# One transformer layer on one core: dense sums read out by two engines, reciprocals over 128 rows

## The chip, the core and the metric

The kernel runs on one core of a Trainium2 chip. A core has a matrix engine (TensorE, PE in the profile; its weight loads are PEld), a vector engine (VectorE, DVE), a scalar engine (ScalarE, ACT), GpSimd (POOL) and SyncE (SP), which issues the transfers here. Matrix products land in PSUM, eight banks of 128 x 512 numbers of four bytes. The metric is the device time of one execution in microseconds (us). Before the change the median of three runs was 1553.09 us (1552.69 to 1554.96).

## The reference: what is computed

A layer with attention and a feed-forward part side by side, for 2048 tokens of width 512:

```python
def _A_ref(x, wqkv, wo):
    qkv = (x @ wqkv).reshape(B, S, 3, H, Dh)...      # 32 heads of 16
    scores = einsum("bhqd,bhkd->bhqk", q, k) * (Dh ** -0.5)
    o = einsum("bhqk,bhkd->bhqd", softmax(scores), v)
    return o... @ wo

def _B_ref(x, w1, b1, w2, b2):                       # 512 -> 1792 -> 512
    h = gelu(einsum("bsd,df->bsf", x, w1) + b1)      # tanh form
    return einsum("bsf,fd->bsd", h, w2) + b2

xn = layernorm(x)
return x + _A_ref(xn, wqkv, wo) + _B_ref(xn, w1, b1, w2, b2)
```

## The kernel before, in words

**Attention.** Work is cut into *units* (`unit`). A tile t is one group of 4 heads and one block of 512 queries, 32 tiles in all; it has 16 units, 512 in all. A unit makes, for four heads, one 128 x 512 block of scores twice. `s_half` computes scores with queries on rows, and VectorE takes their row maximum (`mt`, L250). `e_half`, 20 units later, computes them with keys on rows and the maximum folded in, and ScalarE takes the exponential (`pe`, L295). `v_half` multiplies the exponentials with the values (`pV`). So a unit costs VectorE four maxima and ScalarE four exponentials. At the end of a tile `s_end` turns the maxima into two rows for the next step (L261, L271, L272), and `v_end` copies the sums out (`osb`, L321, ScalarE); their denominators go to memory and come back spread over rows (`dn`), VectorE takes reciprocals (L339), and they return, spread over the rows of `rb`, for GpSimd to multiply.

**Banks.** The scores for the maxima go round through three PSUM banks (tag S), those for the exponentials through three (T). One bank holds the running sums of a dense product (D) and one those of the values (V). At the end of a dense product its bank joins the T banks, and the next product takes one of theirs. TensorE can write a bank only after its reader is through.

**The feed-forward part** is fitted into the units as *groups* of dense products (`Group`, `dense`), each ending in one 128 x 512 block of sums in one bank. There are four blocks of 512 tokens. Each has 14 groups of the first layer (12 products each; by turns 4 units and 3 units long), whose sums VectorE reads out, scaled and with the bias, as `hh` (L992); GpSimd and ScalarE make the gelu of it (`gelu`; the tanh is L961, ScalarE). Then come 4 groups of the second layer (42 products each, 14 units long; 12 in the last block), whose sums ScalarE reads out, scaled, as `yt` (L1008); GpSimd adds them up. In all there are 56 readouts `hh` and 16 `yt`. In the trace the first layer of block 0 runs from 316 to 441 us and its second layer up to 587 us.

**Order.** Each engine works through its list in the order in which the program writes it (`manual_schedule` over all five engines). `later(n, ...)` puts a piece of work n units further on; `pooled` feeds GpSimd's list at a fixed pace per unit. A group's end (`ended`) is written right after the half unit that brought its last product. Waits between engines are put in by the layer below the kernel, from which tiles an instruction reads and writes. `given` only keeps a count which nothing reads.

Of the kernel before, what the change touches and what calls it, by code (L numbers as in the profile page):

```python
# [8 lines left out]
F32 = mybir.dt.float32  # L9
F16 = mybir.dt.float16  # L10
I32 = mybir.dt.int32
AF = mybir.ActivationFunctionType
ALU = mybir.AluOpType
# [4 lines left out]
P = 128  # L18
# [25 lines left out]
W = 2 * P  # L44
# [3 lines left out]
def layer_kernel(ctx: ExitStack, tc: tile.TileContext, x, wqkv, wo, w1, b1, w2, b2, out):  # L48
    nc = tc.nc
# [3 lines left out]
    def pool(stack, name, bufs=1, space=None, side=None):  # L53
        kw = {k: v for k, v in (("space", space), ("side", side)) if v is not None}
        return stack.enter_context(tc.tile_pool(name=name, bufs=bufs, **kw))

    const = pool(ctx, "const")
    work = pool(ctx, "work")
# [11 lines left out]
    den_d = dram.tile([NG * NQB, 2, 4, QB], F32, name="den_d")  # L70
# [88 lines left out]
    def given(engine, ns):  # L159
        backlog[engine] += ns  # L160
# [43 lines left out]
    def later(n, fn, local=False):  # L204
        queue.append((slot[0] + n, fn, local))
# [10 lines left out]
    def pooled(*todo):  # L216
        steps.extend(todo)
# [93 lines left out]
    def v_end(u):  # L311

        t, kt = divmod(u, 16)
        g, qb = divmod(t, NQB)
        for h in range(4):
            del ptiles[u, h]
        if kt < 15:
            return
        pv, k = pv_of.pop(t)
        osb = work.tile([P, QB], F32, name="osb", bufs=2)  # L320
        nc.scalar.activation(osb, pv, AF.Copy)  # L321
        given("act", 600)
        free_banks["S"].append(k)
        if t == NG * NQB - 1:
            later(1, lambda: last_one(osb))
            return

        dn = work.tile([64, 32], F32, name="dn", bufs=1)
        rb = work.tile([P, QB], F32, name="rb", bufs=1)

        def sums():
            for h in range(4):
                nc.sync.dma_start(den_d[t, 0, h:h + 1, :], osb[32 * h + DH:32 * h + DH + 1, :])

        def turned():
            nc.sync.dma_start(dn, den_d[t, 0].rearrange("h (c q) -> (h c) q", q=32))

        def inverse():
            nc.vector.reciprocal(dn, dn)  # L339
            given("dve", 330)  # L340

        def keep():
            nc.sync.dma_start(den_d[t, 1].rearrange("h (c q) -> (h c) q", q=32), dn)

        def spread():
            for h in range(4):
                nc.sync.dma_start(rb[32 * h:32 * h + 32, :], den_d[t, 1, h:h + 1, :].to_broadcast([32, QB]))

        def store():
            ot = work.tile([P, 2, QB], F16, name="ot", bufs=2)  # L350
            pooled((1280, lambda: nc.gpsimd.tensor_tensor(osb, osb, rb, op=ALU.mult)),  # L351
                   (620, lambda: nc.gpsimd.tensor_scalar(ot[:, 0], osb, 1.0, 0.0, op0=ALU.mult, op1=ALU.add)),
                   (1160, lambda: nc.gpsimd.tensor_tensor(ot[:, 1], osb, ot[:, 0], op=ALU.subtract)),
                   (0, lambda: later(6 if t < (NG - 1) * NQB else 1, put)))

            def put():
                for h in range(4):
                    nc.sync.dma_start(ot_d[64 * g + DH * h:64 * g + DH * h + DH, :, qb * QB:(qb + 1) * QB],
                                      ot[32 * h:32 * h + DH])
                ready.add(t)  # L360


        at = (1, 3, 6, 7, 9, 12) if t < (NG - 1) * NQB else (1, 2, 5, 6, 7, 8)
        for k, fn in zip(at, (sums, turned, inverse, keep, spread, store)):
            later(k, fn)
# [168 lines left out]
    def fetch_x(b):  # L534
        if b < NQB:
            xbs[b] = feed[0].tile([P, 2, NC, QB], F16, name="xb", bufs=1)
            for c in range(NC):
                later(1 + c, lambda c=c: nc.sync.dma_start(xbs[b][:, :, c], xn_d[:, :, c, b * QB:(b + 1) * QB]))

    def fetch_w1(n):  # L540
        if n < NQB * NF:
            wcs[n] = feed[0].tile([P, 2, NC, P], F16, name="wc", bufs=3)
            nc.sync.dma_start(wcs[n], w1_d[n % NF // 2, :, n % 2])
# [91 lines left out]
    with ExitStack() as st1:  # L635
# [245 lines left out]
        gs = const.tile([P, 4], F32, name="gs")  # L881
# [69 lines left out]
    def mlp():  # L951
        m2 = st2p
        w2_s = m2.tile([P, 2, NF, D], F16, name="w2_s")
        b2_b = m2.tile([P, D], F32, name="b2_b")
        done = set()

        def gelu(hh, g, b, f):
            t1 = m2.tile([P, QB], F32, name="t1", bufs=2)

            def tanh():  # L960
                nc.scalar.activation(t1, t1, AF.Tanh, scale=GELU_C * GELU_A)  # L961
                given("act", 600)
                later(1, rest, True)

            def rest():
                pooled((690, lambda: nc.gpsimd.tensor_scalar(t1, t1, 1.0, gs[:, 1:2], op0=ALU.add, op1=ALU.mult)),
                       (1280, lambda: nc.gpsimd.tensor_tensor(t1, t1, hh, op=ALU.mult)),  # L967
                       (620, lambda: nc.gpsimd.tensor_scalar(g[:, 0, f, :], t1, 1.0, 0.0, op0=ALU.mult, op1=ALU.add)),
                       (1160, lambda: nc.gpsimd.tensor_tensor(g[:, 1, f, :], t1, g[:, 0, f, :], op=ALU.subtract)),  # L969
                       (0, lambda: done.add((b, f))))  # L970

            pooled((1040, lambda: nc.gpsimd.tensor_tensor(t1, hh, hh, op=ALU.mult)),  # L972
                   (620, lambda: nc.gpsimd.tensor_scalar(t1, t1, 1.0, 1.0 / GELU_A, op0=ALU.mult, op1=ALU.add)),
                   (1280, lambda: nc.gpsimd.tensor_tensor(t1, t1, hh, op=ALU.mult)),  # L974
                   (0, lambda: later(2, tanh, True)))

        for b in range(NQB):
            xb = xbs[b]
            g = m2.tile([P, 2, NF, QB], F16, name="g", bufs=1)
            for f in range(NF):  # L980
                later(1, lambda n=b * NF + f + 2: fetch_w1(n))
                wc = wcs[b * NF + f]
                if b == 0 and f >= 3:
                    for k in range(f - 3, NF if f == NF - 1 else f - 2):
                        later(2 * (k - f + 3), lambda k=k: nc.sync.dma_start(w2_s[:, :, k], w2_d[:, :, k]))
                if b == 0 and f == 3:
                    nc.sync.dma_start(b2_b, b2[None, :].to_broadcast([P, D]))

                def hidden(hp, g=g, b=b, f=f):
                    hh = m2.tile([P, QB], F32, name="hh", bufs=3)  # L990
                    scale, bias = fac1[0][:, f // 2:f // 2 + 1], b1_s[:, f:f + 1]
                    nc.vector.tensor_scalar(hh, hp, scale, bias, op0=ALU.mult, op1=ALU.add)  # L992
                    given("dve", 700)
                    later(1, lambda: gelu(hh, g, b, f), True)

                yield Group([lambda c=c, i=i, j=j, wc=wc, xb=xb: (wc[:, i, c, :], xb[:, j, c, :])
                             for c in range(NC) for i, j in PAIRS], dbank, hidden, pace=FAST if f % 2 else SLOW)
            for q in range(4):
                t = b * 4 + q
                xa = m2.tile([P, D], F32, name="xa", bufs=2)  # L1000
                if q == 1:
                    fetch_x(b + 1)
                nc.sync.dma_start(xa, x[t * P:(t + 1) * P, :])
                later(3, lambda xa=xa: pooled((1280, lambda: nc.gpsimd.tensor_tensor(xa, xa, b2_b, op=ALU.add))), True)

                def store(yp, xa=xa, t=t):
                    yt = m2.tile([P, D], F32, name="yt", bufs=2)
                    nc.scalar.activation(yt, yp, AF.Copy, scale=gs[:, 2:3])  # L1008
                    given("act", 600)
                    add = lambda: nc.gpsimd.tensor_tensor(xa, xa, yt, op=ALU.add)  # L1010
                    put = lambda: nc.sync.dma_start(acc_d[t * P:(t + 1) * P, :], xa)
                    later(1, lambda: pooled((1280, add), (0, lambda: later(4, put, True))), True)

                yield Group([lambda f=f, i=i, j=j, q=q, g=g: (g[:, i, f, q * P:(q + 1) * P], w2_s[:, j, f, :])
                             for f in range(NF) for i, j in PAIRS], dbank, store,
                            lambda n, b=b: (b, n // 3) in done, pace=SLOW if b < 3 else MEAN)
# [126 lines left out]
```

## Time and profile before

| | us |
|---|---|
| median of 3 runs | 1553.09 |
| profiled execution | 1552.32 |
| its span | 1550.5 |
| TensorE busy | 1509.9 (97%) |
| VectorE busy | 1423.0 (92%) |
| ScalarE busy | 1368.6 (88%) |
| GpSimd busy | 652.7 (42%) |

The granted TensorE clock was 0.998 over the span. A row of a timeline gives the start of the first instruction and the length of the whole row, in us from the span's start; then engine, line, operation, what it writes and reads, and how many instructions of one kind the row holds; in brackets, idle time of the engine before it and what ended that. Instructions of one engine overlap a little: the next one starts before the last one's end. So the time for which an instruction holds its engine is the distance to the next start, not its length. In a table of groups the figures behind the bar are busy time in us and the mean length in ns, then idle time before.

### The profile page before, as it was taken

How to read it: one execution, taken by the hardware profiler on the slowest of the kernel's cores; microseconds unless marked ns; L12 is line 12 of the kernel's file. 1: busy time of each engine (PE TensorE's matmuls, PEld its weight loads, DVE VectorE, ACT ScalarE, POOL GpSimd, SP SyncE). 2: the span in 40 equal slices, each digit the busy share in tenths (PEclk: the TensorE clock that was granted, in tenths of full speed). 3: DMA queues.
4: the chain of work that ended last, by engine and by line, in shares of the span. 5: the costliest groups of instructions: out<-in, count | busy, mean ns of one | idle time of the engine just before them, and what ended most of it. 6: DMA issues, size and time to landing. Idle time of an engine off the chain costs nothing.

```text
span 1550.5 us, 85812 instructions
## 1 busy us (share of the span) xinstructions
PE 1509.9 (97%) x38915; PEld 811.2 (52%) x38915; DVE 1423.0 (92%) x2420; ACT 1368.6 (88%) x2254; POOL 652.7 (42%) x678
## 2 busy tenths in 40 slices
PE   8999999999999999999999999999999999999998
PEld 3434555555555555555555555555555555554443
DVE  7899989899999999999999999999999999999701
ACT  4417989999999999999999999999999999999882
POOL 3113797457761114777111277731106775111000
PEclk9999999999999999999999999999999999999999
DMA  6454576442122201121101211121112111102143
GB/s 208 126 158 142 176 233 212 155 120 69 56 63 68 63 21 46 42 76 42 56 27 46 60 42 40 41 83 34 29 35 72 47 35 29 30 30 70 57 139 113
DMA packets 113654, 123.70 MB, mean 80 GB/s; under 512 B 24972, under 2 KB 85260, under 8 KB 113288
## 3 DMA queue, kind: packets, MB, share of 16 engines
q1 hardware_dynamic: 113288, 118.21, 24.8%
q8 instruction: 304, 4.98, 1.3%
q14 instruction: 62, 0.51, 0.1%
HBM read 80.61 MB, written 37.34 MB: 76 GB/s over the span
## 4 chain that ended last, share of the span: by engine, by line
PE 73%; DVE 19%; issue 2%; DMA 2%; SPq 1%; ACT 1%; POOL 1%; DVEq 0%; ACTq 0%; POOLq 0%
PE pV L169 22%; PE pD L169 17%; PE pS L169 15%; PE pT L169 15%; DVE mt L250 14%; DVE hh L992 2%; PE pD L428 1%; PE pT L428 1%; SPq L394 1%; DVE amx L656 1%; DMA m_d<-mhl 1%; DMA oc<-ot_d 1%; PE pT L521 1%; PE pV L521 0%; PE pS L428 0%
## 5 line engine op out<-in xcount | busy, mean ns | idle before, releaser
L295 ACT ACTIVATE pe<-pT,sexp 128x512 f32<-128x512 f32 x2048 | 1267.2, 688 | 66.9 <-PE pT L169 22.4
L250 DVE TENSOR_REDUCE mt<-pS 128x1 f32<-128x512 f32 x2048 | 1287.5, 682 | 31.8 <-PE pS L169 19.7
L169 PE MATMUL pV<-pe,vv 64*32 64x512 f32 x8192 | 1077.8, 596 | 1.0 <-PE pS L169 0.5
L169 PE MATMUL pT<-qst,kst 64*32 64x512 f16 x8192 | 707.6, 378 | 3.2 <-issue 1.8
L169 PE MATMUL pS<-kst,qst 62*32 62x512 f16 x8192 | 635.7, 378 | 17.9 <-DVE mt L250 13.2
L169 PEld LDWEIGHTS <-qst 62*32 62x32 f16 x8192 | 275.9, 92 | 245.7 <-issue 112.1
L169 PEld LDWEIGHTS <-kst 64*32 64x32 f16 x8192 | 301.1, 91 | 182.6 <-issue 76.5
L169 PE MATMUL pD<-w_s,g 64*32 64x512 f16 x5376 | 367.7, 376 | 0.0
L169 PE MATMUL pD<-xb,wc 64*32 64x512 f16 x5376 | 360.5, 377 | 0.0
L169 PEld LDWEIGHTS pV<-pe,vv 64*32 64x32 f32 x8192 | 179.7, 105 | 97.3 <-PE pD L169 7.6
L169 PEld LDWEIGHTS <-wc 64*32 64x32 f16 x5376 | 119.9, 91 | 52.4 <-issue 1.9
L351 POOL TENSOR_TENSOR osb<-osb,rb 128x512 f32<-128x512 f32 x31 | 39.8, 1285 | 234.1 <-DMA rb<-den_d 123.7
L1010 POOL TENSOR_TENSOR xa<-xa,yt 128x512 f32<-128x512 f32 x16 | 20.4, 1278 | 278.9 <-ACT yt L1008 278.9
L169 PEld LDWEIGHTS <-g 64*32 64x32 f16 x5376 | 110.7, 91 | 45.3 <-issue 0.6
L169 PE MATMUL pD<-xt,wqk_h 64*32 64x512 f16 x1920 | 127.1, 378 | 2.0 <-issue 2.0
L972 POOL TENSOR_TENSOR t<-hh 128x512 f32<-128x512 f32 x56 | 58.2, 1039 | 138.7 <-DVE hh L992 138.7
L974 POOL TENSOR_TENSOR t<-t,hh 128x512 f32<-128x512 f32 x56 | 71.7, 1281 | 4.7
L967 POOL TENSOR_TENSOR t<-t,hh 128x512 f32<-128x512 f32 x56 | 71.6, 1278 | 4.7
L969 POOL TENSOR_TENSOR g<-t,g 128x512 f16<-128x512 f32 x56 | 65.2, 1164 | 4.7
L169 PE MATMUL pD<-wo_s,oc 64*32 64x512 f16 x768 | 52.4, 388 | 4.7 <-DMA oc<-ot_d 4.7
L1031 DVE SCALAR_TENSOR_TENSOR ac<-pD,gs,ac 128x512 f32<-128x512 f32 x12 | 9.0, 751 | 48.8 <-PE pT L169 23.9
L169 PEld LDWEIGHTS <-wqk_h 64*32 64x32 f16 x1920 | 43.6, 92 | 17.8 <-issue 2.6
(137 smaller groups left out, 851.9 us busy)
## 6 DMA issues: line engine op xcount, KB each, us to landing
wch<-in_B_w_dram SPq DMA_DIRECT2D x28, 512.0 KB
wc<-w_d SPq DMA_DIRECT2D x56, 256.0 KB
qk_d<-stg SPq DMA_DIRECT2D x32, 256.0 KB
rb<-den_d SPq DMA_DIRECT2D x124, 64.0 KB
w_d<-wsp SPq DMA_DIRECT2D x28, 256.0 KB
kst<-qk_d SPq DMA_DIRECT2D x128, 48.0 KB
qst<-qk_d SPq DMA_DIRECT2D x128, 48.0 KB
xs<-in_A_x_dram SPq DMA_DIRECT2D x16, 256.0 KB
```

The costliest lines, as they stand in the source:

```text
L169: p = nc.tensor.matmul(*args, **kw)
L250: nc.vector.reduce_max(mt_of[t][:, n, qt, kb:kb + 1], s, axis=AX.X)
L295: nc.scalar.activation(pe, st, AF.Exp, scale=sexp[:, g // 2:g // 2 + 1])
L351: pooled((1280, lambda: nc.gpsimd.tensor_tensor(osb, osb, rb, op=ALU.mult)), (620, lambda: nc.gpsimd.tensor_scalar(ot[:, 0], osb, 1.0, 0.0 ...
L394: nc.sync.dma_start((qst, kst)[w][g % 2][p][b][64 * a:64 * a + 48, :], qk_d[w, h * DH:(h + 1) * DH, :, b * QB:(b + 1) * QB].rearrange("d j ...
L428: nc.tensor.matmul(self.bank, lhs, rhs, start=start, stop=self.last and self.over())
L967: (1280, lambda: nc.gpsimd.tensor_tensor(t1, t1, hh, op=ALU.mult)),
L969: (1160, lambda: nc.gpsimd.tensor_tensor(g[:, 1, f, :], t1, g[:, 0, f, :], op=ALU.subtract)),
L972: pooled((1040, lambda: nc.gpsimd.tensor_tensor(t1, hh, hh, op=ALU.mult)), (620, lambda: nc.gpsimd.tensor_scalar(t1, t1, 1.0, 1.0 / GELU_A ...
L974: (1280, lambda: nc.gpsimd.tensor_tensor(t1, t1, hh, op=ALU.mult)),
L992: nc.vector.tensor_scalar(hh, hp, scale, bias, op0=ALU.mult, op1=ALU.add)
L1010: add = lambda: nc.gpsimd.tensor_tensor(xa, xa, yt, op=ALU.add)
```

## The change

Three edits. The readout of the first layer's sums is cut in two: VectorE reads columns 0 to 255, ScalarE columns 256 to 511 (`W` is 256), with the same scale and bias per row. The readout of the second layer's sums is cut in the same way: ScalarE keeps columns 0 to 255, VectorE takes the others. The denominators come back as 128 rows of 16 numbers in place of 64 rows of 32.

```diff
-        dn = work.tile([64, 32], F32, name="dn", bufs=1)
+        dn = work.tile([P, 16], F32, name="dn", bufs=1)
...
         def turned():
-            nc.sync.dma_start(dn, den_d[t, 0].rearrange("h (c q) -> (h c) q", q=32))
+            nc.sync.dma_start(dn, den_d[t, 0].rearrange("h (c q) -> (h c) q", q=16))
...
         def keep():
-            nc.sync.dma_start(den_d[t, 1].rearrange("h (c q) -> (h c) q", q=32), dn)
+            nc.sync.dma_start(den_d[t, 1].rearrange("h (c q) -> (h c) q", q=16), dn)
...
                 def hidden(hp, g=g, b=b, f=f):
                     hh = m2.tile([P, QB], F32, name="hh", bufs=3)
                     scale, bias = fac1[0][:, f // 2:f // 2 + 1], b1_s[:, f:f + 1]
-                    nc.vector.tensor_scalar(hh, hp, scale, bias, op0=ALU.mult, op1=ALU.add)
-                    given("dve", 700)
+                    nc.vector.tensor_scalar(hh[:, :W], hp[:, :W], scale, bias, op0=ALU.mult, op1=ALU.add)
+                    nc.scalar.activation(hh[:, W:], hp[:, W:], AF.Identity, bias=bias, scale=scale)
                     later(1, lambda: gelu(hh, g, b, f), True)
...
                 def store(yp, xa=xa, t=t):
                     yt = m2.tile([P, D], F32, name="yt", bufs=2)
-                    nc.scalar.activation(yt, yp, AF.Copy, scale=gs[:, 2:3])
-                    given("act", 600)
+                    nc.scalar.activation(yt[:, :W], yp[:, :W], AF.Copy, scale=gs[:, 2:3])
+                    nc.vector.tensor_scalar_mul(yt[:, W:], yp[:, W:], gs[:, 2:3])
```

The lists of TensorE and, but for the shape of `dn`, SyncE stay as they were; GpSimd's list keeps its instructions in their order. In ScalarE's list, around the ends of two groups of the first layer in block 0, before (pe are the exponentials, t_... the tile of the tanh; the counter that an instruction waits for stands in brackets, by the name of the engine that raises it):

```order
L961 ACTIVATE t_8468<-t_8468 128x512 [waits Pool_49]
L295 ACTIVATE pe<-pT,sexp 128x512 [waits PE_49,Activation_49]
L295 ACTIVATE pe<-pT,sexp 128x512 [waits PE_49] x3
L295 ACTIVATE pe<-pT,sexp 128x512 [waits PE_49,Activation_49]
L295 ACTIVATE pe<-pT,sexp 128x512 [waits PE_49] x3
L295 ACTIVATE pe<-pT,sexp 128x512 [waits PE_49,Activation_49]
L295 ACTIVATE pe<-pT,sexp 128x512 [waits PE_49] x3
```

and after the change, with the ScalarE halves of two readouts (L993; pD are the dense sums) in it:

```order
L993 ACTIVATE hh<-pD,b_s,fac_2409 128x256 [waits DVE_49]
L961 ACTIVATE t_8470<-t_8470 128x512 [waits Pool_49]
L295 ACTIVATE pe<-pT,sexp 128x512 [waits PE_49,Activation_49]
L295 ACTIVATE pe<-pT,sexp 128x512 [waits PE_49] x3
L295 ACTIVATE pe<-pT,sexp 128x512 [waits PE_49,Activation_49]
L295 ACTIVATE pe<-pT,sexp 128x512 [waits PE_49] x3
L295 ACTIVATE pe<-pT,sexp 128x512 [waits PE_49,Activation_49]
L295 ACTIVATE pe<-pT,sexp 128x512 [waits PE_49] x3
L993 ACTIVATE hh<-pD,b_s,fac_2409 128x256 [waits DVE_49]
L295 ACTIVATE pe<-pT,sexp 128x512 [waits PE_49,Activation_49]
L295 ACTIVATE pe<-pT,sexp 128x512 [waits PE_49] x3
L961 ACTIVATE t_8848<-t_8848 128x512 [waits Pool_49]
```

Each L993 stands ahead of the exponentials, or of the tanh and the exponentials, that came next before; it waits for VectorE's counter alone, at the value to which VectorE's half of the same readout raises it.

In VectorE's list, around the end of a group of the second layer in block 0 (mt are the maxima, dn the denominators, mneg the end of a tile), as a difference:

```order
 L250 TENSOR_REDUCE mt<-pS 128x1 [waits PE_49] x44
-L339 RECIPROCAL dn<-dn 64x32 [waits DMAHW5_49,DMAHW4_49]
-L250 TENSOR_REDUCE mt<-pS 128x1 [waits PE_49] x16
+L339 RECIPROCAL dn<-dn 128x16 [waits DMAHW5_49,DMAHW4_49]
+L250 TENSOR_REDUCE mt<-pS 128x1 [waits PE_49] x8
+L1009 TENSOR_SCALAR yt<-pD,gs 128x256 [waits Activation_49]
+L250 TENSOR_REDUCE mt<-pS 128x1 [waits PE_49] x8
 L261 TENSOR_REDUCE mneg_119<-mt 128x16 [waits DVE_49]
```

VectorE's half of yt (L1009) now stands between the maxima and waits for ScalarE's counter, at the value to which ScalarE's half of the same readout (L1008) raises it.

## The prediction

> **What bounds the kernel now.** I read the page's chain of waits first, then the timelines of single engines at the ends of dense groups.
>
> ```profile
> span 1550.5 us, 85812 instructions
> ...
> PE 73%; DVE 19%; issue 2%; DMA 2%; SPq 1%; ACT 1%; POOL 1%; DVEq 0%; ACTq 0%; POOLq 0%
> PE pV L169 22%; PE pD L169 17%; PE pS L169 15%; PE pT L169 15%; DVE mt L250 14%; DVE hh L992 2%; PE pD L428 1%; PE pT L428 1%; SPq L394 1%; DVE amx L656 1%; DMA m_d<-mhl 1%; DMA oc<-ot_d 1%; PE pT L521 1%; PE pV L521 0%; PE pS L428 0%
> ```
>
> TensorE holds 73% of the chain, VectorE 19%, ScalarE 1%. The profiled execution took 1552.32 us, 1.8 us more than its span and 0.8 us less than the median of the runs shown (1553.09); the sum below starts from 1552.3, and the median comes 0.8 above it.
>
> The price of a readout can be seen in VectorE's timeline. A unit of attention has four row maxima (mt). Where nothing else comes between, and from the first readout hh of block 0 to the last:
>
> ```profile
> 798.21 8.38 DVE L250 TENSOR_REDUCE mt<-pS 128x1 f32<-128x512 f32 x13 [0.30 <-PE pS L169]
> ```
>
> ```profile
> 316.43 0.81 DVE L992 TENSOR_SCALAR hh<-pD,fac,b_s 128x512 f32<-128x512 f32 x1
> ...
> 441.08 0.81 DVE L992 TENSOR_SCALAR hh<-pD,fac,b_s 128x512 f32<-128x512 f32 x1
> ```
>
> ```profile
> 477.60 0.69 ACT L1008 ACTIVATE yt<-pD,gs 128x512 f32<-128x512 f32 x1
> ...
> 586.84 0.69 ACT L1008 ACTIVATE yt<-pD,gs 128x512 f32<-128x512 f32 x1
> ```
>
> Thirteen maxima cover twelve steps and one length: (8.38 - 0.69) / 12 = 0.641 us, so a bare unit takes 2.563. Between the two hh lie 13 groups in 45 units (seven of 3, six of 4): 124.65 us, of which 45 x 2.563 = 115.3, so 9.3 are lost. Between the two yt lie three groups in 42 units: 109.24 - 107.6 = 1.6 lost. If a yt loses 0.28 (next part), the 2.6 ends of attention tiles in that stretch lose (1.6 - 0.84) / 2.6 = 0.29 each; 2.8 of them in the first stretch lose 0.8, which leaves (9.3 - 0.8) / 13 = **0.65 us lost per readout hh**.
>
> **The change, part by part.** The list of the changed program settles one thing no trace shows: the two halves are not read at once. ScalarE's half of hh (L993) waits for the counter of VectorE, at the value that VectorE's half of the same sums raises it to, and VectorE's half of yt (L1009) waits likewise for ScalarE's (rows under the change above). So each end of a group holds two engines, one behind the other, and in ScalarE's queue the exponentials stand behind the wait, for which TensorE waits through the three T banks. The Trainium skill (PSUM — Partial Sum Buffer, section "PSUM bank collisions raise a hardware error") says why such a wait belongs there: two engines that read one bank and quadrant together collide, also on disjoint columns. No run here shows a collision; by that rule the wait can't be dropped, and no form of this split reads one sum from both engines at the same time.
>
> *The halves' lengths.* Groups by shape:
>
> ```profile
> L321 ACT ACTIVATE osb<-pV 128x512 f32<-128x512 f32 x32 | 19.1, 598 | 3.5 <-issue 3.5
> L1008 ACT ACTIVATE yt<-pD,gs 128x512 f32<-128x512 f32 x16 | 11.1, 691 | 0.0
> L145 ACT ACTIVATE wvh<-wch,inv 128x1024 f16<-128x1024 f32 x2 | 2.2, 1187 | 0.0
> L145 ACT ACTIVATE wqk_h<-wq,inv 128x512 f16<-128x512 f32 x1 | 0.7, 722 | 4.2 <-DVE inv L140 4.2
> ```
>
> ```profile
> L733 DVE TENSOR_TENSOR xt<-pT,xt 128x512 f16<-128x512 f32 x7 | 4.8, 686 | 1.6 <-ACT xt L727 1.6
> L376 DVE TENSOR_TENSOR on<-pS,rden 128x256 f32<-128x256 f32 x1 | 0.4, 425 | 0.0
> ```
>
> 256 columns less save VectorE 686 - 425 = 0.26 us, and ScalarE (1187 - 722) / 2 = 0.23. What they hold their engines for is the distance to the next start:
>
> ```profile
> 758.78 0.69 ACT L1008 ACTIVATE yt<-pD,gs 128x512 f32<-128x512 f32 x1
> 759.36 4.86 ACT L295 ACTIVATE pe<-pT,sexp 128x512 f32<-128x512 f32 x8
> ```
>
> ```profile
> 758.86 0.69 DVE L250 TENSOR_REDUCE mt<-pS 128x1 f32<-128x512 f32 x1
> ...
> 761.62 3.27 DVE L250 TENSOR_REDUCE mt<-pS 128x1 f32<-128x512 f32 x5 [0.28 <-PE pS L169]
> ```
>
> ```profile
> 373.49 0.39 PE L169 MATMUL pD<-xb,wc 64*32 64x512 f16 x4
> ```
>
> ```profile
> 374.26 0.63 ACT L961 ACTIVATE t<-t 128x512 f32<-128x512 f32 x1
> 374.78 2.42 ACT L295 ACTIVATE pe<-pT,sexp 128x512 f32<-128x512 f32 x4
> ```
>
> ```profile
> 374.34 0.81 DVE L992 TENSOR_SCALAR hh<-pD,fac,b_s 128x512 f32<-128x512 f32 x1
> 375.07 3.07 DVE L250 TENSOR_REDUCE mt<-pS 128x1 f32<-128x512 f32 x5
> ```
>
> A yt holds ScalarE 0.58 (758.78 to 759.36), an hh VectorE 0.73 (374.34 to 375.07). The half of hh on VectorE is thus 0.73 - 0.26 = 0.47 of holding and 0.81 - 0.26 = 0.55 long. ScalarE's half of hh: 0.58 - 0.23 = 0.35 as a yt is, up to 0.44 if its second operand per row costs what the first does (691 - 598 = 0.09); I take 0.40. The Trainium skill (ScalarE: Activation LUTs, section "What ACT_TABLE_LOAD costs") gives about 93 ns for each such operand, and the 0.09 agrees; by its figures the half would be an estimated 0.49 of holding, and the sum about 5 us higher.
>
> *What a held ScalarE costs.* The yt of 0.58 makes VectorE idle 0.28 three maxima later, for sums that TensorE brings late: ScalarE has 0.30 of slack there. That is the 0.28 used above.
>
> *What waiting adds.* The dense sums are ready at 373.88 (373.49 + 0.39), but VectorE comes to them only at 374.34, behind its maxima; ScalarE is free at 374.26. The handing over, from the rows
>
> ```profile
> 12.44 0.16 DVE L140 RECIPROCAL inv<-fac 128x2 f32<-128x2 f32 x1
> ...
> 12.64 0.72 ACT L145 ACTIVATE wqk_h<-wq,inv 128x512 f16<-128x512 f32 x1 [4.15 <-DVE inv L140]
> ```
>
> is 0.04. ScalarE then begins at 374.34 + 0.55 + 0.04 = 374.93 and is free at 375.33: held for 1.07 us, of which 0.30 is slack. Lost: 0.77, where 0.65 is lost today; VectorE's own 0.47 lies inside it. **+0.12** each.
>
> *With a tanh behind it.* Of the 56 halves in ScalarE's list, 19 have a tanh (L961) right behind, 30 one unit (four exponentials) behind, 7 further. Today that tanh runs under VectorE's readout, as at 374.26. Afterwards its 0.52 (374.26 to 374.78) queues behind the wait: 1.59 - 0.30 = 1.29, **+0.64** for 19. One unit behind, ScalarE has won back only 2.56 - 4 x 0.577 = 0.25 (0.577 from the four exponentials above, (2.42 - 0.69) / 3), so the tanh loses between nothing and 0.27; I take **+0.13** for 30, the middle.
>
> *yt.* ScalarE's half ends at 758.78 + 0.69 - 0.23 = 759.24, VectorE's begins at 759.28 and holds it for 0.47, so the maximum due at 758.86 starts at 759.75, 0.89 late. An hh makes it 0.73 late and loses 0.65 (slack 0.08), while a reciprocal costs nothing at all:
>
> ```profile
> 464.90 0.69 DVE L250 TENSOR_REDUCE mt<-pS 128x1 f32<-128x512 f32 x1
> ...
> 467.36 0.34 DVE L339 RECIPROCAL dn<-dn 64x32 f32<-64x32 f32 x1
> 467.62 3.08 DVE L250 TENSOR_REDUCE mt<-pS 128x1 f32<-128x512 f32 x5
> ...
> 470.01 0.69 DVE L250 TENSOR_REDUCE mt<-pS 128x1 f32<-128x512 f32 x1
> ```
>
> Two units with it take 5.11, two bare ones 5.13: slack up to 0.26. So the yt loses 0.63 to 0.81, today 0.28: +0.35 to +0.53; I take **+0.45**, the middle.
>
> *Reciprocals.* Half the columns save at most 0.13 of a 0.26 which, by these rows, the slack hides; at most 31 x 0.09 = 2.8 us where one follows an hh. The transfers that carry them have as many bytes in twice the rows, and GpSimd, their reader, is busy 42% of the span. I take 0.
>
> *Sum.* 37 x 0.12 = 4.4, 19 x 0.64 = 12.2, 30 x 0.13 = 3.9, 16 x 0.45 = 7.2: 27.7 us. 1552.3 + 27.7 = 1580.0, as a median **1581 us**. Its own bounds: below, VectorE comes 0.18 earlier to the sums (it runs ahead when ScalarE is what delays), the half holds 0.35 and the tanh behind is free: -0.11, +0.41, 0, +0.35 give 9 us, 6 with the reciprocals' gain (1559). Above, 0.44 held and 0.10 more for handing over (a yt's +0.60), the tanh at 0.27: +0.26, +0.78, +0.27, +0.60 give 42 us (1595).
>
> **The rivals.** *ScalarE's slack is gone.* The 0.30 was read in the stage of yt, where no tanh comes; if in the stage of hh the tanh's have spent it, each of the 56 ends loses 0.30 more: 17 us, 1598. For it: both tanh and half now fall into one unit in 19 groups. Against it: four exponentials win back 0.25 per unit, and two units or more lie between.
>
> *VectorE's relief decides (the other side).* If TensorE notices ScalarE's lateness only after 1.07 us, because the same readout holds it back anyway, what counts is VectorE's 0.73 cut to 0.47: 56 x 0.26 = 14.6 us gained, less nothing at the yt: 1538. For it: the tanh at 374.26 puts ScalarE 0.52 late today, at no visible price. Against it: a yt of 0.58 alone costs 0.28, and the wait alone is longer than that.
>
> *The prices cancel.* If ScalarE reached the sums only after VectorE's half ended, the wait would cost nothing, ScalarE's 0.40 would meet 0.30 of slack, and gain at hh would meet loss at yt: about 1550 to 1556. Against it stand 374.26 and 374.93.
>
> **How the numbers follow.** Forecast 0.74; slack gone 0.13; relief decides 0.08; cancel 0.05. The range 1557 to 1599 takes in the forecast's bounds and the first rival. What a measurement of this kernel can tell from no change is about 0.2%, 3 us. Faster by more: the relief and a third of the last, 0.09. Same: 0.04. Slower: 0.87.
>
> **What would show it.** Rows for ScalarE's hh of some 0.5 us that begin about 0.6 us after VectorE's, with idle time before them released by VectorE; idle time of VectorE before L1009 released by ScalarE; TensorE waiting for exponentials, and maxima with idle time before them behind each group's end; blocks of hh (316 to 441 before) about 5 us longer and stretches of yt about 2 us. The prediction is wrong if ScalarE's hh starts with VectorE's, if the readouts stand back to back and the block of hh is still not longer, or if the loss lies in the transfers of the reciprocals.

## The result, and the profile after

The changed kernel takes 1589.95 us (median of 5 runs, 1588.62 to 1591.63) against 1553.09 before in the same comparison: the ratio is 1.0237, with a 95% interval of 1.0221 to 1.0253. It is 36.9 us slower, where 27.7 were forecast; the direction was as forecast, and the time lies inside the range (1557 to 1599).

The page of the changed kernel (busy time, the chain that ended last, and the group of ScalarE's halves):

```profile
span 1588.1 us, 85879 instructions
...
PE 1540.7 (97%) x38915; PEld 815.2 (51%) x38915; DVE 1419.2 (89%) x2436; ACT 1388.5 (87%) x2310; POOL 653.2 (41%) x678
...
PE 73%; DVE 14%; ACT 9%; issue 3%; DMA 1%; POOL 0%; SPq 0%; DVEq 0%; ACTq 0%; POOLq 0%
...
L993 ACT ACTIVATE hh<-pD,b_s,fac 128x256 f32<-128x256 f32 x56 | 31.7, 567 | 30.1 <-DVE hh L992 29.9
```

Two things can be read from it. VectorE and ScalarE are busy for 4 us less and 20 us more, of a span that is 37.6 us longer, so added work alone does not make up the loss. (TensorE is busy for 30.8 us more with the same 38915 products, at a granted clock of 0.997 where it was 0.998; the ends of its products are modelled in the profile, so this is not read as more work.) And ScalarE holds 9% of the chain where it held 1%, VectorE 14% where it held 19%. The last row says what stands in between: ScalarE sat idle for 29.9 us before its 56 halves, until VectorE's half was through. The table of waits of the changed kernel has the wait at both places, and TensorE's wait for the exponentials, which was 0.4 us in one place before:

```profile
ACT hh L993 <- DVE hh L992: 29.9, 52, 0.9
...
PE pT L169 <- ACT pe L295: 10.5, 27, 0.5
...
DVE yt L1009 <- ACT yt L1008: 7.8, 16, 0.6
...
PE pT L169 <- ACT hh L993: 0.2, 1, 0.2
```

The columns are the total in us, how often, and the longest. TensorE's figure counts only stretches in which it had nothing at all under way, so it is no measure of the loss. The last row is TensorE waiting for ScalarE's half itself, because of the bank that it reads: one place, 0.2 us.

Where the time went in block 0: the first and the last readout hh, and the first and the last yt, in the timelines of VectorE and ScalarE.

```profile
317.58 0.54 DVE L992 TENSOR_SCALAR hh<-pD,fac,b_s 128x256 f32<-128x256 f32 x1
...
449.20 0.54 DVE L992 TENSOR_SCALAR hh<-pD,fac,b_s 128x256 f32<-128x256 f32 x1
```

```profile
486.30 0.48 ACT L1008 ACTIVATE yt<-pD,gs 128x256 f32<-128x256 f32 x1
...
597.31 0.48 ACT L1008 ACTIVATE yt<-pD,gs 128x256 f32<-128x256 f32 x1
```

131.62 us where 124.65 stood: 7.0 us for 13 groups, 0.54 for each hh. 111.01 where 109.24 stood: 0.59 for each yt. Times 56 and 16 this is 30.0 + 9.4 = 39.4, about the whole. The prediction had named about 5 us for the first stretch and about 2 for the second.

How one end of a group looks now, first ScalarE, then VectorE, in a place with no tanh near:

```profile
407.32 0.68 ACT L295 ACTIVATE pe<-pT,sexp 128x512 f32<-128x512 f32 x1
408.62 0.57 ACT L993 ACTIVATE hh<-pD,b_s,fac 128x256 f32<-128x256 f32 x1 [0.62 <-DVE hh L992]
409.09 2.42 ACT L295 ACTIVATE pe<-pT,sexp 128x512 f32<-128x512 f32 x4
```

```profile
405.37 0.69 DVE L250 TENSOR_REDUCE mt<-pS 128x1 f32<-128x512 f32 x1
...
408.05 0.54 DVE L992 TENSOR_SCALAR hh<-pD,fac,b_s 128x256 f32<-128x256 f32 x1
408.50 2.47 DVE L250 TENSOR_REDUCE mt<-pS 128x1 f32<-128x512 f32 x4
411.34 0.69 DVE L250 TENSOR_REDUCE mt<-pS 128x1 f32<-128x512 f32 x1 [0.36 <-PE pS L169]
```

ScalarE begins 0.03 us after VectorE's half ends (408.05 + 0.54 = 408.59), and the exponentials come 0.47 later. VectorE itself has its maxima through early and then stands idle for 0.36 us, because TensorE brings the next scores late. From one start of a unit (405.37) to the one two units later (411.34) are 5.97 us, 0.84 more than two bare units (5.13). With a tanh behind the half:

```profile
379.02 0.57 ACT L993 ACTIVATE hh<-pD,b_s,fac 128x256 f32<-128x256 f32 x1 [0.57 <-DVE hh L992]
379.49 0.62 ACT L961 ACTIVATE t<-t 128x512 f32<-128x512 f32 x1
380.01 3.67 ACT L295 ACTIVATE pe<-pT,sexp 128x512 f32<-128x512 f32 x6
```

```profile
375.87 0.69 DVE L250 TENSOR_REDUCE mt<-pS 128x1 f32<-128x512 f32 x1
...
378.44 0.54 DVE L992 TENSOR_SCALAR hh<-pD,fac,b_s 128x256 f32<-128x256 f32 x1
...
382.29 1.29 DVE L250 TENSOR_REDUCE mt<-pS 128x1 f32<-128x512 f32 x2 [0.92 <-PE pS L169]
```

Here two units take 6.42 us, 1.29 more than two bare ones. The exponentials begin at 380.01, 1.57 us after VectorE's half started (378.44).

The same two units, from the fourth maximum ahead of a readout to the fifth behind it, can be measured in the kernel before. Round the readout at 374.34:

```profile
371.79 0.69 DVE L250 TENSOR_REDUCE mt<-pS 128x1 f32<-128x512 f32 x1
...
377.46 0.68 DVE L250 TENSOR_REDUCE mt<-pS 128x1 f32<-128x512 f32 x1
```

These are 5.67 us, so 0.54 are lost. Over all the places where VectorE has nothing but maxima beside the readout, the mean loss is 0.59 before (38 places). After the change it is 0.78 where no tanh stands right behind the half (27 places; the one at 408.62 is among the dearer) and 1.24 where one does (11 places).

### The profile page after: what moved, and what is told of

Read it like the earlier page. It is cut to its first block, busy times and chain, and to the rows that moved or that the text cites. A ratio compares the mean times of both kernels' runs of the same rounds, so it can differ in the third digit from the quotient of the medians.

```text
span 1588.1 us, 85879 instructions
## 1 busy us (share of the span) xinstructions
PE 1540.7 (97%) x38915; PEld 815.2 (51%) x38915; DVE 1419.2 (89%) x2436; ACT 1388.5 (87%) x2310; POOL 653.2 (41%) x678
## 4 chain that ended last, share of the span: by engine, by line
PE 73%; DVE 14%; ACT 9%; issue 3%; DMA 1%; POOL 0%; SPq 0%; DVEq 0%; ACTq 0%; POOLq 0%
PE pV L169 22%; PE pT L169 16%; PE pD L169 16%; PE pS L169 15%; DVE mt L250 10%; ACT pe L295 6%; DVE hh L992 1%; PE pD L428 1%; ACT t L961 1%; PE pT L428 1%; ACT hh L993 1%; DVE amx L656 1%; PE pT L521 1%; ACT yt L1008 0%; DVE yt L1009 0%
## 5 line engine op out<-in xcount | busy, mean ns | idle before, releaser
L169 PE MATMUL pT<-qst,kst 64*32 64x512 f16 x8192 | 719.1, 378 | 14.5 <-ACT pe L295 10.5
L169 PEld LDWEIGHTS <-kst 64*32 64x32 f16 x8192 | 309.4, 91 | 254.1 <-issue 150.9
L169 PEld LDWEIGHTS <-qst 62*32 62x32 f16 x8192 | 267.4, 92 | 214.9 <-issue 87.7
L169 PEld LDWEIGHTS <-wc 64*32 64x32 f16 x5376 | 113.7, 91 | 44.0 <-issue 2.0
L993 ACT ACTIVATE hh<-pD,b_s,fac 128x256 f32<-128x256 f32 x56 | 31.7, 567 | 30.1 <-DVE hh L992 29.9
```

The lines of the kernel that those rows point to most:

```text
L169: p = nc.tensor.matmul(*args, **kw)
L993: nc.scalar.activation(hh[:, W:], hp[:, W:], AF.Identity, bias=bias, scale=scale)
```

## The experiments

Four theories were set against each other. **W**: the wait costs, with what queues behind it. **L**: ScalarE's load costs, the wait matters little. **T**: the new shape of the reciprocals and their transfers costs. **B** (later): TensorE waits for the bank of the dense sums, not for the exponentials. All runs start from the kernel before, unless it is said otherwise.

**Only the split of hh.**

```diff
-nc.vector.tensor_scalar(hh, hp, scale, bias, op0=ALU.mult, op1=ALU.add)
+nc.vector.tensor_scalar(hh[:, :W], hp[:, :W], scale, bias, op0=ALU.mult, op1=ALU.add)
+nc.scalar.activation(hh[:, W:], hp[:, W:], AF.Identity, bias=bias, scale=scale)
```

> Only the readouts hh are split (56 of them, VectorE first, ScalarE waiting for it); yt and the reciprocals stay as before. Theory W (the wait: the second engine stands until the first is through with the sums, and its queue with it): the four blocks of hh cost 7.0 us more each, as in the changed kernel, so 28 to 30 us more than before, some 1582. Theory L (the load: ScalarE has more work than it has room for, the wait itself matters little) says the same here, since both are in. Theory T (the transfers and the shape of the reciprocals): at most 10 us more than before, the rest comes with the reciprocals.

Measured: 1581.84 us, 29.1 over before; ratio 1.0183 (1.0166 to 1.0200). As W and L have it; most of the loss is here.

**Only the split of yt.**

```diff
-nc.scalar.activation(yt, yp, AF.Copy, scale=gs[:, 2:3])
+nc.scalar.activation(yt[:, :W], yp[:, :W], AF.Copy, scale=gs[:, 2:3])
+nc.vector.tensor_scalar_mul(yt[:, W:], yp[:, W:], gs[:, 2:3])
```

> Only the 16 readouts yt are split (ScalarE first, VectorE waiting for it). By the prediction's step +0.35 to +0.53 each, 6 to 8 us over before: 1559 to 1561. If VectorE's slack hides the wait: within 2 us of before.

Measured: 1561.2 us, 7.3 over before; ratio 1.0048 (1.0032 to 1.0064). The step's price holds. In the timeline of VectorE in the changed kernel it looks like this:

```profile
523.96 0.48 DVE L1009 TENSOR_SCALAR yt<-pD,gs 128x256 f32<-128x256 f32 x1 [0.44 <-ACT yt L1008]
524.36 3.07 DVE L250 TENSOR_REDUCE mt<-pS 128x1 f32<-128x512 f32 x5
```

0.44 us idle for ScalarE's half, then 0.40 of holding, with the maxima behind both.

**Only the reciprocals.**

```diff
-dn = work.tile([64, 32], F32, name="dn", bufs=1)
+dn = work.tile([P, 16], F32, name="dn", bufs=1)
...
-"h (c q) -> (h c) q", q=32
+"h (c q) -> (h c) q", q=16
```

> Only the reciprocals' shape: 128 rows of 16. By the prediction's step nothing, -2.8 to +1 us against before, since the slack of VectorE hides them already. Theory T (the transfers with twice the rows delay something): 2 us or more slower.

Measured: 1553.66 us; ratio 1.000 (0.999 to 1.001). T falls. The group of this kernel shows that the instruction did get shorter, 242 ns where it was 334, and that this buys nothing:

```profile
L339 DVE RECIPROCAL dn<-dn 128x16 f32<-128x16 f32 x31 | 7.5, 242 | 0.0
```

The three parts add up to 29.1 + 7.3 - 0.3 = 36.1 us, the whole change to 36.9.

**The split of hh without the wait.** VectorE's half gets another source, so that no two engines read the sums.

```diff
-nc.vector.tensor_scalar(hh[:, :W], hp[:, :W], scale, bias, op0=ALU.mult, op1=ALU.add)
+nc.vector.scalar_tensor_tensor(hh[:, :W], vv[:, 0, :W], scale, vv[:, 1, :W], op0=ALU.mult, op1=ALU.add)
 nc.scalar.activation(hh[:, W:], hp[:, W:], AF.Identity, bias=bias, scale=scale)
```

> As the split of hh alone, but VectorE's half is made from 256 columns of a tile in SBUF (the values' tile, scaled and added, about as long) and not from the dense sums, so that ScalarE's half waits for TensorE alone; half of hh is thus not the layer's. Both engines hold what they held. Theory W: the wait of 0.6 us is gone; VectorE's 0.47 loses about 0.3 per group, ScalarE's 0.47 plus a tanh right behind about 0.7 in 19 groups: 29 us lost over 56 groups where 36 are lost before, so 1540 to 1556, no slower than before. Theory L: the load is as in the split of hh alone, so the time is within 6 us of it (1576 to 1588).

Measured: 1552.7 us; ratio 0.9996 (0.9982 to 1.0009). Groups of this kernel, first VectorE's, then ScalarE's:

```profile
L992 DVE SCALAR_TENSOR_TENSOR hh<-vv,fac 128x256 f32<-128x256 f32 x56 | 29.2, 521 | 0.0
```

```profile
L993 ACT ACTIVATE hh<-pD,b_s,fac 128x256 f32<-128x256 f32 x56 | 31.9, 569 | 0.0
```

The halves are about as long as in the split with the wait (543 and 564 ns there), the idle time before ScalarE's is zero, and 29 us are gone. Both halves still go into one tile `hh`, so the wait came with the sums that both read and not with the tile that both write. L falls, and the time lies in W's range, but the 7 us that W's sum would gain are not there. As far as this stand-in goes (its VectorE half need not wait for the sums either), the split in this order of the lists would gain nothing even without the wait. The places show why: over the two units 0.26 us are lost where no tanh stands right behind (27 places), but 0.65 where one does (11), and the unit that follows on a tanh one unit behind loses 0.30 (19 places) where it loses nothing before the change. VectorE's relief is spent on the tanh.

**The other order.** ScalarE's half is written first, VectorE waits for it.

```diff
+nc.scalar.activation(hh[:, W:], hp[:, W:], AF.Identity, bias=bias, scale=scale)
 nc.vector.tensor_scalar(hh[:, :W], hp[:, :W], scale, bias, op0=ALU.mult, op1=ALU.add)
-nc.scalar.activation(hh[:, W:], hp[:, W:], AF.Identity, bias=bias, scale=scale)
```

> The split of hh alone with the halves in the other order: ScalarE reads its half first, VectorE waits for it. Same work on each engine. Theory W: the maxima now stand behind the wait; ScalarE's half ends at 0.57 after it is free, VectorE's then holds 0.47, so the next maximum comes 1.0 late, 0.83 to 0.9 lost in each of the 56 groups where 0.65 is lost before and 1.0 to 1.3 with VectorE first; a tanh right behind hides in that. So 10 to 16 us over before: 1563 to 1569, clearly under the split with VectorE first. Theory L: ScalarE's load is the same, so the time is that of the split with VectorE first within 4 us.

Measured: 1572.42 us; ratio 1.0122 (1.0104 to 1.0140). 9 us under the split with VectorE first, at the same work, as W has it, though 3 us over W's figure. The wait has moved, into VectorE's queue (waits of this kernel):

```profile
DVE hh L993 <- ACT hh L992: 35.4, 56, 1.0
```

A readout costs more there where no tanh stands right behind the half, 1.00 us over the two units (27 places) against 0.78 in the changed kernel; but with a tanh it costs 0.86 (11 places) against 1.24, and the unit that follows on a tanh one unit behind loses nothing (19 places) against 0.36. The tanh no longer queues behind a wait, and that makes this order the cheaper one.

**ScalarE's half later.** VectorE first, and ScalarE's half written two exponentials further on, when VectorE's is over.

```diff
-nc.scalar.activation(hh[:, W:], hp[:, W:], AF.Identity, bias=bias, scale=scale)
+held.append(lambda: nc.scalar.activation(hh[:, W:], hp[:, W:], AF.Identity, bias=bias, scale=scale))
...
+            while held:
+                held.pop(0)()
             if e >= 0:
                 enter()
```

> The split of hh alone, VectorE first, but ScalarE's half is written two exponentials later, when VectorE's half is over, so that ScalarE need not stand and wait. All the layer is computed. Theory W: VectorE's 0.47 loses about 0.3, ScalarE's half fits into its slack or loses up to 0.3 beside a tanh: about 25 us lost over the 56 groups where 36 are lost before: 1538 to 1548, 5 to 15 us faster than before. Theory L: same load on ScalarE as in the split of hh alone, so 1576 to 1588.

Measured: 1591.97 us; ratio 1.0247 (1.0231 to 1.0262). Both theories missed: 10 us worse than the split with the wait, where W had forecast a gain on before. The waits of this kernel show why (its lines are numbered one to three higher, L996 is ScalarE's half, L170 the products):

```profile
PE pT L170 <- ACT hh L996: 41.6, 56, 1.1
```

All 56 times TensorE now waits for the late half itself, as it did once in the changed kernel. When a dense product ends, its bank goes to the exponentials' scores, which take it one half unit later. An early half keeps the exponentials waiting, a late half keeps the bank. My expectation had looked at the engines' queues alone. So in the changed kernel, too, the bank might be what is waited for, which the next run takes apart.

**The wait without the bank.** ScalarE's half takes VectorE's finished half in SBUF as its input: it waits as long and does as much, and the bank is free once VectorE is through.

```diff
-nc.scalar.activation(hh[:, W:], hp[:, W:], AF.Identity, bias=bias, scale=scale)
+nc.scalar.activation(hh[:, W:], hh[:, :W], AF.Identity, bias=bias, scale=scale)
```

> As the split of hh alone, VectorE first, but ScalarE's half takes VectorE's finished half in SBUF as its input in place of the dense sums' other columns, so that it waits for VectorE just as long and holds ScalarE as long, while the dense sums' bank is free when VectorE's half is through; half of hh is thus not the layer's. Theory W as the prediction priced it (the exponentials queued behind the wait keep TensorE from the T banks): 1578 to 1585, as the split of hh alone. Theory B (what TensorE waits for is the dense sums' own bank, which it takes for the next scores): the bank comes free 0.6 us earlier in each of 56 groups; the 37 without a tanh behind fall back to about VectorE's 0.3 us lost: 1555 to 1568.

Measured: 1586.8 us; ratio 1.0212 (1.0190 to 1.0234). Groups of ScalarE in this kernel, then its waits:

```profile
L993 ACT ACTIVATE hh<-hh,b_s,fac 128x256 f32<-128x256 f32 x56 | 33.6, 600 | 30.8 <-DVE hh L992 30.6
```

```profile
PE pT L169 <- ACT pe L295: 21.0, 60, 0.7
```

Freeing the bank 0.6 us earlier gives nothing back; the half from SBUF is 33 ns longer than that of the changed kernel, and the time a little over W's 1578 to 1585. B falls for the split as it was made: TensorE waits for the exponentials, and the bank would decide only if the half came later.

**All of hh on ScalarE.**

```diff
-nc.vector.tensor_scalar(hh, hp, scale, bias, op0=ALU.mult, op1=ALU.add)
+nc.scalar.activation(hh, hp, AF.Identity, bias=bias, scale=scale)
```

> The readouts hh whole on ScalarE, none on VectorE: no wait between engines, twice the changed kernel's work on ScalarE. Theory W: held 0.47 + 0.21 = 0.68 less 0.30 of slack is 0.38 lost in 37 groups, 0.90 in the 19 with a tanh behind, and 0.28 for 30 tanh one unit behind: 40 us where 36 are lost before, so 1550 to 1562, some 20 us under the split. Theory L (ScalarE's load is what costs): more load than the split, so 1582 or more.

Measured: 1563.69 us; ratio 1.0066 (1.0047 to 1.0085). Its group:

```profile
L992 ACT ACTIVATE hh<-pD,b_s,fac 128x512 f32<-128x512 f32 x56 | 43.8, 782 | 0.0
```

215 ns more on ScalarE for each readout than the split has, and 18 us less: no engine waits for another. L falls a second time. W's range ended at 1562, so it is 2 us over it.

**Another cut.** 384 columns on VectorE, which is first, 128 on ScalarE.

```diff
-hh[:, :W], hp[:, :W]  ...  hh[:, W:], hp[:, W:]
+hh[:, :W + P], hp[:, :W + P]  ...  hh[:, W + P:], hp[:, W + P:]
```

> The split of hh alone at 384 columns for VectorE, which is first, and 128 for ScalarE. Theory W: the one waits for the other, so the time from the sums' readiness to the end of the second half is nearly the same wherever the cut lies (VectorE 0.13 longer, ScalarE 0.11 shorter): 1578 to 1586, as the split in the middle. Theory L: ScalarE has 0.11 less to do in each of 56 groups, most of which come back: 1574 to 1577.

Measured: 1585.65 us; ratio 1.0207 (1.0191 to 1.0223), W's figure. ScalarE's half:

```profile
L993 ACT ACTIVATE hh<-pD,b_s,fac 128x128 f32<-128x128 f32 x56 | 25.6, 458 | 38.2 <-DVE hh L992 38.2
```

It is 109 ns shorter than the 256 columns of the changed kernel, and ScalarE waits for it 8 us longer in all. Moving the cut moves work from one engine to the other; the sum of the two in a row stays.

**Without the tanh, after and before.** The first starts from the changed kernel, the second from the one before.

```diff
-nc.scalar.activation(t1, t1, AF.Tanh, scale=GELU_C * GELU_A)
```

> The changed kernel without the 56 tanh instructions of ScalarE (the gelu is left without its tanh, GpSimd goes on as before). Theory W with the tanh queued behind the wait, as the after trace reads: 19 tanh right behind a half cost 0.52 each, 30 one unit behind 0.28 each: 18 us less than the changed kernel, about 1572. If the tanh costs nothing there: 1588 to 1590.

> The kernel before without the 56 tanh instructions (the gelu is left without its tanh). If the tanh runs under VectorE's readout before, as the prediction says, this is 0 to 4 us faster than before; if the tanh costs before what it costs after the change, 18 us.

Measured: 1571.66 us after (18.3 under the changed kernel; ratio to before 1.0125, 1.0106 to 1.0144), and 1551.47 before (ratio 0.9986, 0.9976 to 0.9997, 2.5 us). Both as W has it: a tanh that ran nearly free under VectorE's readout costs (18.3 - 2.5) / 56 = 0.28 us more each once it queues behind the wait.

No version that computes the whole layer beats the kernel before.

## Why the prediction was right, and where its sizes were off

**Not at once.** The step that carried the forecast, that the two halves would stand one behind the other, is what the trace shows: 29.9 us idle before L993 and 7.8 before L1009, in 52 and 16 places. Without this wait the split costs nothing (0.9996). The handing over was put at 0.04 and is 0.03. The Trainium skill (PSUM — Partial Sum Buffer, section "PSUM bank collisions raise a hardware error") has two engines collide that read one bank and quadrant at the same time; no run here read one bank from two engines at the same time, so that was not tried.

**The readouts hh.** By the sum a half without a tanh loses 0.77 us, and one with a tanh right behind 1.29; the means are 0.78 and 1.24. That the first is met so well is partly luck. ScalarE's holding, taken as 0.40 between bounds of 0.35 and 0.44, is 0.47 (408.62 to 409.09), outside these bounds. At the place shown ScalarE is free at 407.90 (407.32 and 0.58 for the exponential) and held until 409.09, 1.19 us where the sum had 1.07; but 0.84 is lost there, so the slack is 0.35 where the sum had 0.30. Both sizes were too small, and they work against each other. The bound was built from one operand per row more (0.09) and 256 columns less (0.23, from SBUF rows); three lengths now show 128, 256 and 512 columns at 458, 567 and 782 ns, so 256 columns are (782 - 567) = 0.215. The Trainium skill (ScalarE: Activation LUTs, section "What ACT_TABLE_LOAD costs") had given an estimated 0.49, and the measured 0.47 lies nearer to it than to my bound.

The term that was mis-sized is the one that was taken away: 0.65 lost today, which came from the length of a whole block. Over the same two units it is 0.59, so a half without a tanh costs 0.19 us and not 0.12.

**The tanh.** The 30 that stand one unit behind were priced at half of 0.27, as the middle between nothing and all. The trace shows all of it. At one of them, ScalarE's tanh and then VectorE's first maximum of the unit after:

```profile
390.93 0.65 ACT L961 ACTIVATE t<-t 128x512 f32<-128x512 f32 x1
```

```profile
393.74 0.69 DVE L250 TENSOR_REDUCE mt<-pS 128x1 f32<-128x512 f32 x1 [0.27 <-PE pS L169]
```

Over 19 such places the unit that ends there loses 0.36 us in the changed kernel and 0.09 in the same kernel without the tanh. A tanh right behind, priced at 0.52, costs 1.24 - 0.78 = 0.46. So 19 x 0.46 + 30 x 0.27 = 16.8; the runs without the tanh show 18.3 - 2.5 = 15.8, and the sum had 19 x 0.52 + 30 x 0.13 = 13.8.

Together, per part: the split of hh was put at 4.4 + 12.2 + 3.9 = 20.5 us and costs 29.1. By the runs, the tanh accounts for 15.8 of that where 13.8 were forecast, and the halves alone for 13.3 where 56 x 0.12 = 6.7 were; the 0.19 in place of 0.12 explains 3.9 of the 6.6 missing there. About 2.7 us, 0.05 per readout, stay without a row of their own.

**yt and the reciprocals.** yt: 7.2 forecast, 7.3 measured; one place shows 0.84 us of lateness (0.44 + 0.40) where 0.89 was worked out. Reciprocals: nothing forecast, nothing measured, although the instruction is 92 ns shorter.

**The rivals.** *Slack gone* (1598) overstated: the 0.30 of slack that was read at yt held at hh, or the mean losses would be 1.07 and 1.59 where they are 0.78 and 1.24. *The relief decides* (1538) is refuted most directly by the run without the wait: even there VectorE's shorter half gains nothing, since ScalarE's half and tanh lose it again. *The prices cancel* would have needed ScalarE to come last to the sums; it was idle there 52 times.

One piece of the picture was missing. The prediction spoke of the exponentials' banks and left out that the dense sums' own bank is soon one of them: it takes the third block of scores after the group's end. It did not matter for this change, but it decided the attempt to repair it.

## What to carry to other kernels

Splitting one PSUM block between two engines buys no parallel reading where the readers of a bank are put in sequence: price it as the sum of both halves plus the handing over, and price what queues behind the second engine's wait at nearly its full length (here 0.46 of the tanh's 0.52 us). Before an engine is relieved, look at what runs free under its present delay (here the tanh); it becomes the next cost. A readout has two deadlines, the queue of the engine that does it and the next user of its bank, and moving it later trades the one for the other.

## What was not expected of the hardware

An activation with scale and bias both given per row took 458, 567 and 782 ns for 128, 256 and 512 columns out of PSUM: about 0.84 us per 1000 columns and 0.35 us before the first. So half a readout takes 73% of a whole one, and cutting it in two raises the sum of the pieces: 543 ns on VectorE and 567 on ScalarE stand where one of 809 or of 782 stood. The same activation out of SBUF took 600 ns for 256 columns, 33 more than out of PSUM; that is one kernel, whose half reads what VectorE has just written.
